# A gate broadcast moved behind four transposes, and scale columns regrouped, in a DiT block on one core

## The chip, the cores and the metric

The kernel runs on one core of a Trainium2 chip. The metric is the device time of that core in microseconds.

The engines are called as the profile calls them: PE is the matmul engine, PEld its weight loads, DVE, ACT and POOL the vector, scalar and GpSimd engines, SP the engine that issues most loads.

## The reference, cut to what matters

```python
# B, N, D = 2, 256, 1152; H = 2 heads of 576; F = 4608; all bfloat16
mod = (silu(c) @ w_mod).reshape(B, 6, 1, D)
shift_a, scale_a, gate_a, shift_m, scale_m, gate_m = [mod[:, i] for i in range(6)]
h = layernorm(x) * (1 + scale_a) + shift_a
q, k, v = h @ wqkv                                    # cut: reshapes
attn = softmax(q k^T * Dh ** -0.5)
x = x + gate_a * ((attn @ v) @ wo)
h2 = layernorm(x) * (1 + scale_m) + shift_m
out = x + gate_m * (gelu(h2 @ w_fc1) @ w_fc2)
```

D is nine blocks of 128. "Column j of the scale" below means block j of `scale_a`, which is needed before the normalized activations of block j can be modulated and used in K step j.

## The kernel before

Everything is resident or streamed through five large weight buffers, and PE works from start to end.

**The first loads**, on SP's queue, in the order in which PE will want them: scale columns and rows of the K weights, alternating.

```python
SGROUPS = [(0, 2), (2, 4), (4, 6), (6, 8), (8, 9)]
for k0, k1 in SGROUPS:
    nc.sync.dma_start(w_scale_a[:, :, k0*P:k1*P], ...)     # one load for each group of columns
    for a, z in [(0, 1), (1, 2)] if k0 == 0 else [(k0, k1)]:
        load_k(a, z, 0, KM1 * P)                           # rows of the K weights
load_k(0, KD, KM1 * P, D)
```

**The K steps.** `scale_group` computes columns by small matmuls, `transpose_x` and `modulate` make block k of the activations, `k_step` accumulates it into six PSUM tiles.

```python
k_step(0, N, T)                      # batch 1's half of step 0
pm = scale_group(2, 4)               # waits for the second scale load
pt_b = transpose_x([2, 3], BT[0])
scale_add(pm, 2, 4)
modulate(...)                        # cut: DVE and ACT
k_step(1, N, T)                      # batch 1's half of step 1
...                                  # cut
for k in range(3, KD):
    split = 2 if k == 5 else 0
    k_step(k, 0, T, 0, split)
    if k in (3, 5, 7):
        k1 = min(k + 3, KD)
        scale_add(scale_group(k + 1, k1), k + 1, k1)
    ...                              # cut
```

**Attention.** Four softmaxes end in four DMA transposes on ACT's queue (`transposed` is the last). The gate vector is written to a DRAM tile in four pieces and read back broadcast to 128 partitions, 2 x 288 KB, on POOL's queue. The next weights (`w_shift_m`, `w_scale_m`, `w_f1_0`, a first piece of `w_f1_1`) wait for the last transpose.

```python
def gate_natural_finish(g, pn):
    ...                                            # cut: four small writes to gates_dram
    return broadcast_gate(g)                       # two DMAs, at once
for i, (pnl, t) in enumerate(v_order):
    if i < len(softmaxes):
        transposed = softmaxes[i]()
    if i == 0:
        gate_a = gate_finish()
    v_group(pnl, t)
w_shift_m = load_rows("w_shift_m", ...)
tc.add_manual_dep(first_load["w_shift_m"], transposed.ins.name, WAIT_FOR, reason="transposes first")
w_scale_m = load_rows(...); w_f1[0] = load_rows(...)
for c0, c1 in ((0, PW), (PW, D)):                  # two pieces of w_f1_1; the second waits for LN2
    load = nc.sync.dma_start(w_f1[1][:, :, c0:c1], ...)
```

**The second layernorm (LN2).** Each token tile t is normalized, then turned by a DMA transpose on ACT's queue into `hT`. fc1 of batch 0 needs tiles 0 and 1. It follows the output projection ("wo") on PE directly.

```python
nc.scalar.dma_start_transpose(hT[:, :, t * P:(t + 1) * P], xn2[:])
```

Of the kernel before, what the change touches and what calls it, by code (L numbers as in the profile page):

```python
# [19 lines left out]
def kernel(  # L20
# [11 lines left out]
    nc = tc.nc  # L32
    B, N, D = x.shape
# [3 lines left out]
    P = 128  # L37
    T = B * N
    NT = T // P
    TPB = N // P  # L40
    KD = D // P
# [8 lines left out]
    WAIT_FOR = mybir.DependencyInfo(mybir.DependencyClass.Sync, mybir.DependencyReason.DATA)  # L50
# [9 lines left out]
    def acc_tile(shape, name, dt=FP32):  # L60
        return psum.tile(shape, dt, name=name, tag="acc", bufs=6)
# [16 lines left out]
    def wide_tile(name):  # L78
        return wide.tile([P, KD, D], BF16, name=name, tag="wide")
# [15 lines left out]
    sT = act.tile([P, KD, SW], BF16, name="sT")  # L95
    nc.gpsimd.memset(sT[:], 0.0)

    SGROUPS = [(0, 2), (2, 4), (4, 6), (6, 8), (8, 9)]
    KM1 = 6
    w_scale_a = wide_tile("w_scale_a")  # L100
    w_k = wide_tile("w_k")
# [1 line left out]
    def load_k(k0, k1, c0, c1):  # L103
        nc.sync.dma_start(w_k[:, k0:k1, c0:c1], wqkv_v[:, k0:k1, D + c0:D + c1])

    for k0, k1 in SGROUPS:
        nc.sync.dma_start(
            w_scale_a[:, :, k0 * P:k1 * P],
            wmod_v[:, :, S_SCALE_A * D + k0 * P:S_SCALE_A * D + k1 * P],
        )  # L110
        for a, z in [(0, 1), (1, 2)] if k0 == 0 else [(k0, k1)]:
            load_k(a, z, 0, KM1 * P)
    load_k(0, KD, KM1 * P, D)

# [2 lines left out]
    def load_rows(name, view, col0):  # L117
        w = wide_tile(name)
        for r in range(0, KD, 3):
            load = nc.sync.dma_start(w[:, r:r + 3, :], view[:, r:r + 3, col0:col0 + D])  # L120
            first_load.setdefault(name, load.ins)
        return w
# [109 lines left out]
    def norm1(t, c0, c1):  # L232
        nc.vector.tensor_scalar(
            xns[t][:, c0:c1], x_sb[:, t, c0:c1], mv1[:, t, 0:1], rstd1[:, t:t + 1],
            op0=ALU.subtract, op1=ALU.mult,
        )
# [4 lines left out]
    def scale_group(k0, k1, tile_of=aux_tile):  # L241
        pm = tile_of([P, k1 - k0, B], "pm")
        for j in range(k0, k1):
            if j == 0:
                nc.tensor.matmul(pm[:, 0, :], ones_row[:], ones_row[:, 0:B], start=True, stop=False)
            for k in range(KD):
                nc.tensor.matmul(  # L247
                    pm[:, j - k0, :], w_scale_a[:, k, j * P:(j + 1) * P], sT[:, k, 0:B],
                    start=(k == 0 and j > 0), stop=(k == KD - 1),
                )  # L250
        return pm

    def scale_add(pm, k0, k1, eng="d"):
        if eng == "a":
            nc.scalar.activation(scale_a[:, k0:k1, :], pm[:], ACT.Identity, bias=ones[:])
        else:
            nc.vector.tensor_scalar_add(scale_a[:, k0:k1, :], pm[:], 1.0)

    def transpose_x(ks, ts, pt=None, j0=0):
        if pt is None:  # L260
            pt = aux_tile([P, len(ks), len(ts) * P], "pt", BF16)
        for j, t in enumerate(ts, j0):
            for i, k in enumerate(ks):
                nc.tensor.transpose(pt[:, i, j * P:(j + 1) * P], xns[t][:, k * P:(k + 1) * P], ident[:])  # L264
        return pt
# [10 lines left out]
    def k_step(k, c0=0, c1=T, m0=0, m1=KM1):  # L276
        for m in range(m0, m1):
            if k == 0 and c0 == 0:
                pk[m] = acc_tile([P, T], "pk")
            nc.tensor.matmul(  # L280
                pk[m][:, c0:c1], w_k[:, k, m * P:(m + 1) * P], hT0[:, k, c0:c1],
                start=(k == 0 and c0 == 0), stop=(k == KD - 1), skip_group_check=True,
            )
# [33 lines left out]
    def both(pt, k):  # L317
        for b, e in enumerate("da"):
            modulate(pt, 0, k, b, b * N, e)
# [60 lines left out]
    norm1(0, CUT, D)  # L380
    norm1(1, CUT, D)
    k_step(0, N, T)
    pm = scale_group(2, 4)
    pt_b = transpose_x([2, 3], BT[0])
    scale_add(pm, 2, 4)
    modulate(pt_b, 0, 2, 0, 0, "d")
    modulate(pt_b, 1, 3, 0, 0, "a")
    norm1(2, CUT, D)
    k_step(1, N, T)
    pt_d = transpose_x([2, 3], BT[1])  # L390
    modulate(pt_d, 0, 2, 1, 0, "d")
    modulate(pt_d, 1, 3, 1, 0, "a")
    norm1(3, CUT, D)
    k_step(2, 0, N)
    k_step(2, N, T)
    for k in range(3, KD):
        split = 2 if k == 5 else 0
        k_step(k, 0, T, 0, split)
        if k in (3, 5, 7):
            k1 = min(k + 3, KD)  # L400
            scale_add(scale_group(k + 1, k1), k + 1, k1)
        if k < KD - 1:
            both(transpose_x([k + 1], range(NT)), k + 1)
        k_step(k, 0, T, split)
# [45 lines left out]
    nc.vector.tensor_reduce(fold[:], ident[:].rearrange("p (q a) -> p a q", a=32), axis=AX.X, op=ALU.add)  # L450
    gates_dram = tc.dram_tile([2, B, D], BF16, name="gates_dram")

    def broadcast_gate(g):
        gate = act.tile([P, B, D], BF16, name="gate", tag="gate")
        for b in range(B):
            nc.gpsimd.dma_start(gate[:, b, :], gates_dram[g, b:b + 1, :].partition_broadcast(P))
        return gate


# [23 lines left out]
    def gate_vector_finish(g, folded):  # L483
        rows = D // 32
        pg = aux_tile([rows, B, 32], "pg")
        for b in range(B):
            nc.tensor.matmul(pg[:, b, :], folded[:, b, :], fold[:], start=True, stop=True)
        nat = work.tile([rows, B, 32], BF16, name="nat_v", tag="nat_v", bufs=1)
        nc.vector.tensor_copy(nat[:], pg[:])  # L489
        for b in range(B):  # L490
            nc.gpsimd.dma_start(gates_dram[g, b, :].rearrange("(j r) -> j r", r=32), nat[:, b, :])  # L491
        return broadcast_gate(g)

    def gate_natural(g, wg):
        pn = aux_tile([P, CTW], "pg")
        for k in range(KD):
            for i in range(4):
                nc.tensor.matmul(  # L498
                    pn[32 * i:32 * i + B, :], sT[:, k, 0:B], wg[:, k, i * CTW:(i + 1) * CTW],
                    start=(k == 0), stop=(k == KD - 1), tile_position=(0, 32 * i),  # L500
                )
        return lambda: gate_natural_finish(g, pn)

    def gate_natural_finish(g, pn):
        nat = work.tile([P, CTW], BF16, name="nat", tag="nat", bufs=1)
        for i in range(4):
            rows = slice(32 * i, 32 * i + B)
            if i % 2 == 0:
                nc.vector.tensor_copy(nat[rows, :], pn[rows, :])  # L509
            else:  # L510
                nc.scalar.copy(nat[rows, :], pn[rows, :])
            nc.gpsimd.dma_start(gates_dram[g, :, i * CTW:(i + 1) * CTW], nat[rows, :])  # L512
        return broadcast_gate(g)


    pq = [None] * KD
# [54 lines left out]
    gate_finish = gate_natural(0, w_gate_a)  # L571
# [24 lines left out]
    def v_group(pnl, t):  # L596
        pacc = acc_tile([P, PW], "pacc")
        for k in range(KD):
            nc.tensor.matmul(  # L599
                pacc[:], hT[:, k, t * P:(t + 1) * P], w_v[:, k, pnl * PW:(pnl + 1) * PW],  # L600
                start=(k == 0), stop=(k == KD - 1),
            )
        evac(v_sb[:, t, pnl * PW:(pnl + 1) * PW], pacc[:])
# [3 lines left out]
    for i, (pnl, t) in enumerate(v_order):  # L607
        if i < len(softmaxes):
            transposed = softmaxes[i]()
        if i == 0:  # L610
            gate_a = gate_finish()
        v_group(pnl, t)

    w_shift_m = load_rows("w_shift_m", wmod_v, S_SHIFT_M * D)
    tc.add_manual_dep(first_load["w_shift_m"], transposed.ins.name, WAIT_FOR, reason="transposes first")
    w_scale_m = load_rows("w_scale_m", wmod_v, S_SCALE_M * D)
    w_f1[0] = load_rows("w_f1_0", wfc1_v, 0)
    w_f1[1] = wide_tile("w_f1_1")
    for c0, c1 in ((0, PW), (PW, D)):
        load = nc.sync.dma_start(w_f1[1][:, :, c0:c1], wfc1_v[:, :, D + c0:D + c1])  # L620
# [172 lines left out]
    for gi, (n, t, c0, cw) in enumerate(groups):  # L793
        b = t // TPB
# [59 lines left out]
```

## Time and profile before

| | before |
|---|---|
| time, median of 3 runs | 243.91 us (243.87 to 244.05) |
| span of the profiled execution | 241.8 us |
| PE busy | 235.4 us |
| first real matmul | 8.8 us |
| last matmul's start | 238.4 us |

From the page of the profile: the span, the busy time by engine, and the chain of work that ended last, as shares of the span by engine.

```profile
span 241.8 us, 3979 instructions
...
PE 235.4 (97%) x1688; PEld 144.4 (60%) x1698; DVE 91.5 (38%) x193; ACT 59.9 (25%) x121; POOL 28.3 (12%) x47
...
PE 94%; issue 2%; ACT 2%; POOL 1%; DVE 0%; POOLq 0%; DVEq 0%; ACTq 0%
```

PE is the bound. The view of windows gives the length of a stretch and the busy time of PE, PEld, DVE, ACT and POOL in it, then the granted clock, the DMA share and GB/s.

```profile
8.80:25.50 16.70, 16.27 (x189) 11.13 (x191) 7.36 (x25) 6.14 (x14) 0.98 (x3) 1.00 1.13 320
56.00:97.70 41.70, 41.70 (x329) 26.32 (x330) 25.48 (x62) 13.57 (x37) 9.86 (x13) 1.00 0.88 272
```

The first row is the stage of scale groups and K steps: 0.43 us are idle. The second row is from the v matmuls to fc1: nothing is idle.

The waits view, for PE alone (who waited for whom: us in total, times, longest):

```profile
PE pt L264 <- DVE xn L233: 1.5, 2, 1.2
PE pwarm L173 <- DVE eps_t L93: 1.2, 1, 1.2
```

No matmul waits for a load. The timeline (start, length, engine, line, operation) shows the weight loads of the second scale group running without a wait:

```profile
12.69 0.61 PEld L247 LDWEIGHTS <-w_scale_a 128*128 128x128 bf16 x18
```

The timeline around the attention transposes: the third and fourth transpose, the two broadcasts, and the load of w_shift_m that waits for the fourth transpose.

```profile
61.33 2.55 ACTq L550 DMA_TRANSPOSE soft<-soft  x2
63.26 1.14 POOL L456 DMA_DIRECT2D gate<-gates_dram  x2 [1.86 <-DMA gates_dram<-nat]
67.06 0.90 SPq L120 DMA_DIRECT2D w_shift_m<-in_w_mod_dram  x2
```

The view of the tile, cut to the fourth transpose, gives its time from issue to landing:

```profile
L550 ACTq DMA_TRANSPOSE soft<-soft x1: 1242/1242/1242, 62.6 to 62.6; - x1
...
DMA to landing us min/median/max: 4.4/4.4/4.4
```

And the timeline where wo ends and fc1 begins: the second LN2 transpose is issued, DVE modulates, PE starts fc1.

```profile
93.66 1.31 ACTq L681 DMA_TRANSPOSE hT<-xn  x1
96.98 0.60 DVE L662 TENSOR_SCALAR hT<-hT,scale_m,shift_m 128x256 bf16<-128x256 bf16 x2 [0.26 <-DMA hT<-xn]
97.62 0.60 PE L743 MATMUL pacc<-hT,w_f 128*128 128x256 bf16 x4
```

PE has no idle time in front of it, as the view of windows shows for this place:

```profile
96.50:98.00 1.50, 1.50 (x12) 1.01 (x11) 1.24 (x5) 1.22 (x4) 0.47 (x1) 1.00 0.00 0
```

### The profile page before, as it was taken

What the parts mean: (1) busy time and instruction counts of PE and PEld (TensorE: products, weight loads), DVE (VectorE), ACT (ScalarE), POOL (GpSimd) and SP (SyncE); (2) the same over time, 40 slices, a digit from 0 to 9 for tenths busy, and PEclk for the clock granted to TensorE, in tenths of its full rate; (3) what the DMA queues carried; (4) which work ended last, traced back from release to release, by engine and by line L of the source; (5) the groups of instructions that cost most, each with busy time, mean ns of one, the idle gap of its engine ahead of it and who ended that gap; (6) DMA issues with size and microseconds to landing.
All of it is one profiled execution on the core that took longest, in us unless ns stands there. A gap on an engine that the chain in (4) does not pass through costs nothing.

```text
span 241.8 us, 3979 instructions
## 1 busy us (share of the span) xinstructions
PE 235.4 (97%) x1688; PEld 144.4 (60%) x1698; DVE 91.5 (38%) x193; ACT 59.9 (25%) x121; POOL 28.3 (12%) x47
## 2 busy tenths in 40 slices
PE   8799999999999999999999999999999999999994
PEld 5585444465567566888844444444556665566674
DVE  3742442319325678830002999960010000000001
ACT  6633322307215032671422333222000000000000
POOL 2300000002300324100000000001121111111111
PEclk9999999999999999999999999999999999999999
DMA  6999999997579999239999999999200000000000
GB/s 188 327 317 310 378 366 393 389 391 247 147 263 398 387 377 159 49 59 361 391 391 391 340 327 284 274 327 284 98 16 16 20 16 16 19 18 19 27 23 16
DMA packets 48781, 53.29 MB, mean 220 GB/s; under 512 B 9587, under 2 KB 36475, under 8 KB 48763
## 3 DMA queue, kind: packets, MB, share of 16 engines
q1 hardware_dynamic: 41312, 50.14, 62.5%
q10 hardware_dynamic: 6939, 1.71, 4.7%
q0 software_dynamic: 512, 1.19, 1.5%
q8 instruction: 13, 0.21, 0.4%
q14 instruction: 5, 0.04, 0.0%
HBM read 50.14 MB, written 1.19 MB: 212 GB/s over the span
## 4 chain that ended last, share of the span: by engine, by line
PE 94%; issue 2%; ACT 2%; POOL 1%; DVE 0%; POOLq 0%; DVEq 0%; ACTq 0%
PE pacc L799 29%; PE pacc L743 29%; PE pacc L690 7%; PE pacc L599 7%; PE pq L521 7%; PE pk L280 5%; PE pk L309 2%; PE pa L639 2%; PE ps_s L556 2%; PE pn L416 2%; ACT sink L206 1%; PE pt L264 1%; PE pm L247 1%; PE pg L498 0%; ACT rstd L335 0%
## 5 line engine op out<-in xcount | busy, mean ns | idle before, releaser
L743 PE MATMUL pacc<-hT,w_f 128*128 128x256 bf16 (+1 forms) x427 | 70.3, 325 | 0.3
L799 PE MATMUL pacc<-w_f,gT 128*128 128x384 bf16 (+2 forms) x468 | 70.5, 314 | 0.0
L799 PEld LDWEIGHTS <-gT 128*128 128x128 bf16 x468 | 44.4, 98 | 26.2
L743 PEld LDWEIGHTS <-w_f 128*128 128x128 bf16 x432 | 42.2, 98 | 27.6
L805 DVE TENSOR_TENSOR tmp<-pacc,gate 128x384 f32<-128x384 f32 (+2 forms) x13 | 6.9, 527 | 65.6 <-PE pacc L799 57.2
L775 ACT ACTIVATE gT<-pacc 128x512 bf16<-128x512 f32 x24 | 14.3, 597 | 32.6 <-PE pacc L743 32.6
L469 DVE SCALAR_TENSOR_TENSOR part<-w_gate_m,s,part 128x1152 f32<-128x1152 bf16 x16 | 21.4, 1414 | 0.0
L807 POOL TENSOR_TENSOR o_sb<-tmp,x 128x384 bf16<-128x384 f32 (+1 forms) x12 | 11.7, 973 | 54.0 <-DVE tmp L805 54.0
L690 PE MATMUL pacc<-w_o,big 128*128 128x384 bf16 x108 | 17.9, 326 | 0.0
L521 PE MATMUL pq<-hT,w_q 128*128 128x512 bf16 x79 | 17.7, 379 | 0.1
L599 PE MATMUL pacc<-w_v,hT 128*128 128x384 bf16 x108 | 17.7, 326 | 0.0
L599 PEld LDWEIGHTS <-hT 128*128 128x128 bf16 x108 | 10.5, 98 | 7.1 <-issue 0.3
L690 PEld LDWEIGHTS <-big 128*128 128x128 bf16 x108 | 10.4, 98 | 7.2 <-issue 0.4
L521 PEld LDWEIGHTS <-w_q 128*128 128x128 bf16 x81 | 7.9, 98 | 9.4
L280 PE MATMUL pk<-big,w_k 128*128 128x256 bf16 (+1 forms) x70 | 13.1, 324 | 0.1
L696 POOL TENSOR_TENSOR x<-tmp,x_sb 128x384 f32<-128x384 f32 x8 | 7.3, 914 | 27.4 <-DVE tmp L695 27.4
L467 DVE TENSOR_SCALAR part<-w_gate_m,s 128x1152 f32<-128x1152 bf16 x2 | 1.6, 818 | 22.3 <-DMA w_gate_m<-in_w_mod_dram 22.3
L491 POOL DMA_DIRECT2D gates_dram<-nat_v x2 | 1.1, 536 | 67.7 <-DVE nat_v L489 67.7
L280 PEld LDWEIGHTS <-w_k 128*128 128x128 bf16 x72 | 6.7, 97 | 3.7 <-issue 0.3
L764 ACT ACTIVATE gT<-pacc 128x512 bf16<-128x512 f32 x12 | 6.5, 598 | 8.9 <-PE pacc L743 8.9
L512 POOL DMA_DIRECT2D gates_dram<-nat x4 | 2.3, 584 | 49.3 <-DVE nat L509 48.7
L695 DVE TENSOR_TENSOR tmp<-pacc,gate 128x384 f32<-128x384 f32 x12 | 6.6, 549 | 3.1 <-PE pacc L690 3.1
(102 smaller groups left out, 164.2 us busy)
## 6 DMA issues: line engine op xcount, KB each, us to landing
w_f<-in_w_fc_dram SPq DMA_DIRECT2D x12, 864.0 KB, 14.9
w_f<-in_w_fc_dram SPq DMA_DIRECT2D x3, 1728.0 KB, 7.9
w_f<-in_w_fc_dram SPq DMA_DIRECT2D x2, 2592.0 KB, 17.2
w_gate_a<-in_w_mod_dram SPq DMA_DIRECT2D x3, 864.0 KB, 11.9
w_v<-in_wqkv_dram SPq DMA_DIRECT2D x3, 864.0 KB, 13.8
w_o<-in_wo_dram SPq DMA_DIRECT2D x3, 864.0 KB, 14.0
w_shift_m<-in_w_mod_dram SPq DMA_DIRECT2D x3, 864.0 KB, 6.6
w_scale_m<-in_w_mod_dram SPq DMA_DIRECT2D x3, 864.0 KB, 12.1
```

Of the source, the lines that this page charges most:

```text
L280: nc.tensor.matmul(pk[m][:, c0:c1], w_k[:, k, m * P:(m + 1) * P], hT0[:, k, c0:c1], start=(k == 0 and c0 == 0), stop=(k == KD - 1), skip_g ...
L469: nc.vector.scalar_tensor_tensor(part[:, b, :], wg[:, k, :], s32[:, k, b:b + 1], part[:, b, :], op0=ALU.mult, op1=ALU.add,)
L521: nc.tensor.matmul(pq[m][:], w_q[:, k, m * P:(m + 1) * P], hT[:, k, :], start=(k == 0), stop=(k == KD - 1), skip_group_check=True,)
L599: nc.tensor.matmul(pacc[:], hT[:, k, t * P:(t + 1) * P], w_v[:, k, pnl * PW:(pnl + 1) * PW], start=(k == 0), stop=(k == KD - 1),)
L690: nc.tensor.matmul(pacc[:], aT[:, k, t * P:(t + 1) * P], w_o[:, k, c0:c1], start=(k == 0), stop=(k == KD - 1),)
L695: nc.vector.tensor_tensor(tmp[:], pacc[:], gate_a[:, b, c0:c1], op=ALU.mult)
L696: (nc.gpsimd if pool_add else nc.vector).tensor_tensor(x1[:, t, c0:c1], tmp[:], x_sb[:, t, c0:c1], op=ALU.add)
L743: nc.tensor.matmul(dst, w_f1[m // KD][:, k, ml * P:(ml + 1) * P], hT[:, k, c0:c1], start=start, stop=(k == KD - 1), **kw,)
L775: nc.scalar.activation(gT[:, m, :], pacc[:], ACT.Gelu_apprx_tanh)
L799: nc.tensor.matmul(pacc[:], gT[:, kk, t * P:(t + 1) * P], w_f2[j][:, r, c0 - n * PW:c0 - n * PW + cw], start=(kk == 0), stop=(kk == KF - 1),)
L805: nc.vector.tensor_tensor(tmp[:], pacc[:], gate_m[:, b, c0:c0 + cw], op=ALU.mult)
L807: (nc.vector if last else nc.gpsimd).tensor_tensor(o_sb[:], tmp[:], x1[:, t, c0:c0 + cw], op=ALU.add)
```

## The change

The intent can be read from the diff. The broadcast no longer shares the DMA engines with the last attention transpose, so the transpose and the loads behind it come earlier. The scale columns come in four loads instead of five, without the narrow last one. Three matmuls go ahead of the second group, whose load is now larger.

```diff
-    SGROUPS = [(0, 2), (2, 4), (4, 6), (6, 8), (8, 9)]
+    SGROUPS = [(0, 2), (2, 5), (5, 7), (7, 9)]
@@
-        for a, z in [(0, 1), (1, 2)] if k0 == 0 else [(k0, k1)]:
+        ends = {0: (1, 2), 2: (3, 5)}.get(k0, (k1,))
+        for a, z in zip((k0,) + ends, ends):
             load_k(a, z, 0, KM1 * P)
@@
     k_step(0, N, T)
+    k_step(1, N, T, 0, 3)
     pm = scale_group(2, 4)
     pt_b = transpose_x([2, 3], BT[0])
@@
-    k_step(1, N, T)
+    k_step(1, N, T, 3)
@@
+    INSIDE = {3: (0, (4, 5)), 4: (2, (5, 7)), 6: (2, (7, 9))}
     for k in range(3, KD):
-        split = 2 if k == 5 else 0
+        split, group = INSIDE.get(k, (0, None))
         k_step(k, 0, T, 0, split)
-        if k in (3, 5, 7):
-            k1 = min(k + 3, KD)
-            scale_add(scale_group(k + 1, k1), k + 1, k1)
+        if group:
+            scale_add(scale_group(*group), *group)
@@
-    def broadcast_gate(g):
+    def broadcast_gate(g, behind=None):
         gate = act.tile([P, B, D], BF16, name="gate", tag="gate")
         for b in range(B):
-            nc.gpsimd.dma_start(gate[:, b, :], gates_dram[g, b:b + 1, :].partition_broadcast(P))
+            load = nc.gpsimd.dma_start(gate[:, b, :], gates_dram[g, b:b + 1, :].partition_broadcast(P))
+            if behind is not None:
+                tc.add_manual_dep(load.ins, behind, WAIT_FOR, reason="transposes first")
+                behind = None
@@ gate_natural_finish
-        return broadcast_gate(g)
@@
-            gate_a = gate_finish()
+            gate_finish()
@@
     tc.add_manual_dep(first_load["w_shift_m"], transposed.ins.name, WAIT_FOR, reason="transposes first")
+    gate_a = broadcast_gate(0, transposed.ins.name)
     w_scale_m = load_rows("w_scale_m", wmod_v, S_SCALE_M * D)
```

## The prediction

> **What bounds it.** TensorE. The page gives PE 235.4 us busy of a 241.8 us span; the chain of waits is 94% PE. After warm-up's start the waits view lists two PE waits, both for normalized activations (1.5 us together), none for a DMA. The rest is the start (first real matmul at 8.82 us) and the tail (3 us). In the stretch 8.8 to 25.5 us, where scale groups and K steps run, PE is busy 16.27 of 16.70 us: at most 0.43 us to give. From 56.0 to 97.7 us PE has no idle time.
>
> **Change 1: scale groups.** All scale columns and K matmuls stay; order and load sizes change. Landings, from issue start plus time to landing: group 2-3 about 12.1 us (interpolated), group 4-5 at 15.26, 6-7 at 18.32, 8 at 21.33. PE's weight loads ask for them at 12.69, 15.55, 19.36, 22.46: slack 0.6, 0.3, 1.0, 1.1 us. Nothing waits today. After: group 2-4 has 864 KB instead of 576; at about 300 KB/us (group 4-5: 576 KB in 1.96 us) it lands near 13.0 us. Three 256-column matmuls (0.33 us in the chain) now go first, so PE asks at about 13.02. Slack shrinks to nearly zero: a stall of 0 to 0.3 us is possible. Later groups gain: 5-6 lands near 16.7, wanted near 18.0; 7-8 near 19.8 against 21.5. The lone column 8 with its 256-byte pieces is gone; it took 1.19 us for 288 KB (242 KB/us, against about 295 for 512-byte pieces). The Trainium skill, "DMA: Bandwidth & Descriptors", Specifications, puts line rate at 512 bytes or more; this trace agrees. That saves about 0.25 us of queue time, off the critical path.
> The moved matmuls leave 0.33 us less cover for the next modulation: VectorE's would end near 14.37, wanted at 14.51. Tight, but no wait.
>
> **Change 2: gate_a.** Now its two broadcasts (issued 63.26 and 63.8 us, landing after 3.6 to 3.8) overlap the last attention transpose, which takes 4.4 us against 2.4 to 2.5 for those before it, and holds w_shift_m's load until 67.06. After: that transpose lands about 2 us earlier, w_shift_m is issued near 65, and the broadcast shares the DMA engines with it, landing near 69 to 71. Its first reader runs at 79.31: 8 us of slack. The broadcast's traffic (about 1.5 us at 390 GB/s) moves into the busy load phase, cancelling most of the 2 us. w_scale_m lands today at 84.2, wanted at 87.6; it should land at most 0.5 us earlier. PE has no idle time here: gain on the span zero.
>
> **Prediction.** 243.9 us, range 243.5 to 244.5. Faster by over 2%: 0.4%; within 2%: 99%; slower: 0.6%.
>
> **What would show it.** Right: PE busy near 235.4; no PE wait for DMA, or one below 0.3 us at the second scale group (12.7 to 13.5 us); last attention transpose under 3 us; w_shift_m issued near 65 us; first gate product still released by PE near 79.3. Wrong: a gate product waiting for the gate; a PE gap above 0.3 us near 13 us; fc1 starting later than 97.6 us plus any shift from the K steps.
>
> **What would make it wrong.** Group 2-4 landing later than 13.3 us, each further 0.1 us adding 0.1; landings in unprofiled runs that differ, so that before really stalls at group 4-5 and after gains some tenths; the broadcast starving behind the load queue; loads running longer into the LN2 transposes before 97 us.

## The result, and the profile after

| | before | after |
|---|---|---|
| time, median of 6 runs | 243.89 us (243.55 to 244.41) | 243.88 us (243.80 to 244.67) |
| ratio, 95% interval | | 1.0003 (0.9986 to 1.0019) |
| span of the profiled execution | 241.8 us | 242.2 us |
| PE busy | 235.4 us | 235.6 us |

A ratio here and below is the mean time of one kernel's fast runs over the mean of the other's fast runs of the same rounds, so it isn't quite the ratio of the medians quoted.

The time is the same. The profile is not: nearly each thing that the change was to do happened. The page:

```profile
span 242.2 us, 3979 instructions
...
PE 235.6 (97%) x1688; PEld 144.1 (60%) x1698; DVE 91.5 (38%) x193; ACT 60.2 (25%) x121; POOL 28.3 (12%) x47
...
PE 91%; issue 2%; ACT 2%; DMA 2%; DVE 1%; POOL 1%; DVEq 0%; POOLq 0%; ACTq 0%
```

The chain of work that ended last now has 2% DMA in it, where before it had none. The windows of the first stretch, and of the place where wo ends and fc1 begins:

```profile
8.80:25.50 16.70, 16.34 (x188) 10.91 (x188) 7.11 (x25) 5.91 (x13) 0.74 (x3) 1.00 1.11 336
96.50:98.00 1.50, 1.39 (x10) 0.76 (x8) 0.71 (x3) 0.98 (x3) 0.50 (x1) 1.00 0.36 78
```

In the first stretch PE is as busy as it was. In the second it is idle for 0.11 us where before had none. (From 56.00 to 97.70 us nothing is idle in this kernel either; that stretch ends just before the gap.) The weight loads of the second scale group now wait for their load, 0.23 us by the timeline, and begin at 13.02 us, close to the 13.0 us that the prediction gave for the larger load's landing:

```profile
13.02 0.52 PEld L248 LDWEIGHTS <-w_scale_a 128*128 128x128 bf16 x18 [0.23 <-DMA w_scale_a<-in_w_mod_dram]
```

(PE itself waits 0.17 us for the first scale load, at 9.26 us; the change leaves that load as it was.)

The attention transposes, w_shift_m's load and the broadcast on the timeline:

```profile
61.36 2.53 ACTq L554 DMA_TRANSPOSE soft<-soft  x2
65.12 1.43 SPq L121 DMA_DIRECT2D w_shift_m<-in_w_mod_dram  x3
65.64 1.14 POOL L458 DMA_DIRECT2D gate<-gates_dram  x2 [4.21 <-DMA soft<-soft]
```

The fourth transpose's time to landing in the view of its tile:

```profile
L554 ACTq DMA_TRANSPOSE soft<-soft x1: 1231/1231/1231, 62.7 to 62.7; - x1
...
DMA to landing us min/median/max: 2.4/2.4/2.4
```

The fourth transpose takes 2.4 us instead of 4.4, and w_shift_m's load goes out 1.94 us earlier. The gate is read for the first time at 79.34 us and is still released by PE, as before.

But the timeline at the start of fc1 has this:

```profile
93.69 1.31 ACTq L686 DMA_TRANSPOSE hT<-xn  x1
...
97.53 0.60 DVE L667 TENSOR_SCALAR hT<-hT,scale_m,shift_m 128x256 bf16<-128x256 bf16 x2 [0.78 <-DMA hT<-xn]
97.92 0.27 PE L748 MATMUL pacc<-hT,w_f 128*128 128x256 bf16 x1
```

The second LN2 transpose was issued 0.03 us later than before and landed at 97.43 instead of 96.88 us. fc1 starts 0.30 us later. That is most of the 0.37 us between the two spans (242.16 and 241.79 us exactly). The question for the experiments is whether that is noise, which part of the change makes it, and why loads that started 2 us earlier end up hurting.

### The profile page after: what moved, and what is told of

Same layout as the page of the kernel before. It is cut to its first block, busy times and chain, and to the rows that moved or that the text cites. A ratio compares the mean times of both kernels' runs of the same rounds, so it can differ in the third digit from the quotient of the medians.

```text
span 242.2 us, 3979 instructions
## 1 busy us (share of the span) xinstructions
PE 235.6 (97%) x1688; PEld 144.1 (60%) x1698; DVE 91.5 (38%) x193; ACT 60.2 (25%) x121; POOL 28.3 (12%) x47
## 3 DMA queue, kind: packets, MB, share of 16 engines
q0 software_dynamic: 512, 1.19, 1.7%
HBM read 50.14 MB, written 1.19 MB: 212 GB/s over the span
## 4 chain that ended last, share of the span: by engine, by line
PE 91%; issue 2%; ACT 2%; DMA 2%; DVE 1%; POOL 1%; DVEq 0%; POOLq 0%; ACTq 0%
PE pacc L804 29%; PE pacc L748 29%; PE pacc L603 7%; PE pq L525 7%; PE pk L281 5%; PE pacc L695 4%; PE pk L310 2%; PE pa L644 2%; PE ps_s L560 2%; DMA hT<-xn 2%; PE pn L418 2%; ACT sink L207 1%; PE pt L265 1%; PE pm L248 1%; PE pg L503 0%
## 5 line engine op out<-in xcount | busy, mean ns | idle before, releaser
L804 PEld LDWEIGHTS <-gT 128*128 128x128 bf16 x468 | 44.3, 98 | 26.3
L603 PEld LDWEIGHTS <-hT 128*128 128x128 bf16 x108 | 10.5, 98 | 7.1 <-issue 0.3
## 6 DMA issues: line engine op xcount, KB each, us to landing
w_o<-in_wo_dram SPq DMA_DIRECT2D x3, 864.0 KB, 13.9
```

The lines of the kernel that those rows point to most:

```text
L603: nc.tensor.matmul(pacc[:], hT[:, k, t * P:(t + 1) * P], w_v[:, k, pnl * PW:(pnl + 1) * PW], start=(k == 0), stop=(k == KD - 1),)
L804: nc.tensor.matmul(pacc[:], gT[:, kk, t * P:(t + 1) * P], w_f2[j][:, r, c0 - n * PW:c0 - n * PW + cw], start=(kk == 0), stop=(kk == KF - 1),)
```

## The experiments

There were twelve runs in three sets of four (e1 to e4; r1, e6, e7, e8; e5, e9, r2, r3), each set on one chip with its own runs of the kernel before. The changed kernel itself was timed again in the second set only, so a comparison of the other two sets with it goes through the ratios to before. Each run had one profile and five rounds. All results were correct.

| run | what it is | ratio to before (95%) | medians, this / before |
|---|---|---|---|
| e1_gate_only | before + gate part | 1.0020 (1.0004 to 1.0036) | 244.05 / 243.63 |
| e2_groups_only | before + groups part | 1.0039 (1.0020 to 1.0058) | 244.65 / 243.63 |
| e3_split_load | after, 864 KB load in two | 1.0029 (1.0015 to 1.0044) | 244.34 / 243.63 |
| e4_no_move | after, three matmuls not moved | 1.0042 (1.0025 to 1.0058) | 244.46 / 243.63 |
| r1_after_again | after, unaltered | 1.0002 (0.9983 to 1.0020) | 243.98 / 243.93 |
| e6_gate_twice | after, broadcast doubled | 1.0043 (1.0020 to 1.0066) | 245.13 / 243.93 |
| e7_late_piece | after, piece of w_f1_1 held | 1.0003 (0.9983 to 1.0024) | 244.10 / 243.93 |
| e8_late_piece_before | before, piece held | 0.9987 (0.9970 to 1.0003) | 243.65 / 243.93 |
| e5_bigger_group | after, second group 1152 KB | 1.0054 (1.0042 to 1.0066) | 244.62 / 243.53 |
| e9_groups_late_piece | groups only, piece held | 1.0007 (0.9995 to 1.0020) | 243.66 / 243.53 |
| r2_groups_again | groups only again | 1.0046 (1.0029 to 1.0062) | 244.58 / 243.53 |
| r3_late_before_again | before, piece held, again | 1.0015 (0.9997 to 1.0033) | 243.76 / 243.53 |

The second table is worked out from the trace of each run, in us. "Loads" is the time from the issue of w_shift_m to the landing of the third piece of w_f1_0. "Lag" is the landing of the second LN2 transpose minus the start of the last wo matmul. "Gap" is the start of the first fc1 matmul minus the start of the last wo matmul, less the 0.16 that remains where nothing waits. The profile's own idle figures, counted from the modelled end of the last matmul, come out about 0.16 us smaller than this gap.

| run | 4th attention transpose | w_shift_m issued | broadcast among the loads | loads | lag | gap |
|---|---|---|---|---|---|---|
| before | 4.37 | 67.06 | no | 23.9 | -0.58 | 0 |
| e8, r3 | 4.31, 4.77 | 67.08, 67.28 | no | 24.2, 24.2 | -0.58, -0.58 | 0, 0 |
| e2, r2 | 5.13, 4.99 | 68.24, 68.49 | no | 24.1, 24.2 | 0.45, 0.63 | 0.79, 0.97 |
| e9 | 5.24 | 67.95 | no | 24.1 | -0.57 | 0 |
| after, r1 | 2.41, 2.41 | 65.12, 64.97 | once | 26.4, 26.3 | -0.06, 0.15 | 0.28, 0.48 |
| e1 | 2.39 | 65.18 | once | 26.2 | -0.34 | 0 |
| e3, e4 | 2.39, 2.41 | 65.31, 65.66 | once | 26.3, 26.5 | -0.32, -0.12 | 0.02, 0.22 |
| e5 | 2.41 | 65.98 | once | 26.3 | 0.37 | 0.70 |
| e7 | 2.41 | 64.80 | once | 26.4 | -0.55 | 0 |
| e6 | 2.41 | 65.30 | twice | 29.4 | 1.24 | 1.58 |

### Each part alone: e1_gate_only and e2_groups_only

e1 takes the gate part of the diff above and leaves the groups. e2 takes the rest; as a diff against the changed kernel:

```diff
@@ gate_natural_finish
+        return broadcast_gate(g)
@@
-            gate_finish()
+            gate_a = gate_finish()
@@
-    gate_a = broadcast_gate(0, transposed.ins.name)
```

> The kernel before with the gate part of the change alone. My theory (each part touches only slack): the last attention transpose lands in 2.4 us instead of 4.4, w_shift_m is issued near 65.1, no scale group waits for a load, the gate is read for the first time at 79.3 still released by PE; time within 0.15% of before. In the changed kernel's profile the second LN2 transpose landed 3.7 us after its issue instead of 3.2 and PE sat 0.27 us before fc1; if the gate's later traffic is the cause, this run has the gap too (0.1 to 0.4 us). Rival A (two real effects that cancel): this run is slower than before by 0.2 to 0.4 us (ratio 1.001 to 1.002) and the groups-only run faster by as much. Rival B (noise of one profile): no gap before fc1 here.

> The changed kernel with gate_a's broadcast where it was before. My theory: PE waits 0.1 to 0.3 us for the load of scale columns 2-4 near 13 us, as in the changed kernel; the last attention transpose takes 4.4 us again and w_shift_m goes out near 67; no gap before fc1 (under 0.05 us); time within 0.15% of before, if anything 0.1 to 0.2 us slower. Rival A: faster than before by 0.2 to 0.4 us. Rival B: a gap before fc1 may show here as well.

My theory held for e1's transpose and lost in most of the rest. e1's fourth transpose took 2.39 us and w_shift_m went out at 65.18, as expected, but PE has no gap before fc1 there, and the ratio, 1.0020, is outside the 0.15% that I gave. It is e2, with the broadcast in its old place, that has the gap, and a larger one. In e2 the transpose took 5.13 us and not 4.4, w_shift_m went out at 68.24 and not near 67, and the ratio was 1.0039. The expected wait at the second scale group did not show in e2: PE came to the group only at 13.42 us. From the timeline of e2:

```profile
94.08 1.33 ACTq L686 DMA_TRANSPOSE hT<-xn  x1
...
98.83 1.03 PE L748 MATMUL pacc<-hT,w_f 128*128 128x256 bf16 x8 [0.62 <-DVE hT L667]
```

Rival A had foreseen two effects of opposite sign, with groups-only the faster one. Both parts alone came out slower than before, by 0.20% (an interval that just excludes 1) and 0.39%. For the changed kernel, which has both, the first measurement's interval (0.9986 to 1.0019) lies below that of groups-only (1.0020 to 1.0058). So the parts aren't a sum: the gate part takes back most of what the groups part loses. Gate-only and the changed kernel can't be told apart. The second table shows where the parts meet. In e2 the fourth attention transpose, with the broadcast beside it, took 5.13 us, w_shift_m went out at 68.24 us, and the loads, which took 24.1 us as before, ended 1.36 us later than before (92.31 against 90.95 us). The LN2 transposes followed them. Of the 1.36 us, 0.42 are not the transpose's: this profile was already late when the v matmuls began (56.35 against 55.93 us). The column "lag" doesn't hold that shift.

### The changed kernel again: r1_after_again

> The changed kernel itself, unaltered, beside before on the chip and in the rounds of the runs below. My theory after the first four runs: before fc1 there is a chain (end of the load queue, then the two LN2 transposes of batch 0, then the first modulation, then PE) with only some 0.2 us of slack in before; the change delays the end of that queue by about 1 us and uses the slack up. So this profile again shows the second LN2 transpose landing about 0.2 us before PE could start, and a PE gap of 0.1 to 0.5 us before fc1; ratio to before between 1.000 and 1.003. Rival (noise of one profile): no gap this time.

The gap came again, larger. From this run's timeline, the start of fc1:

```profile
97.97 1.80 PE L748 MATMUL pacc<-hT,w_f 128*128 128x256 bf16 x15 [0.32 <-DVE hT L667]
```

So it isn't the chance of one profile, and rival B falls. The ratio, 1.0002, repeats the first result, 1.0003.

### What the broadcast costs the loads: e6_gate_twice

```diff
     gate_a = broadcast_gate(0, transposed.ins.name)
+    spare = act.tile([P, B, D], BF16, name="spare", tag="spare")
+    for b in range(B):
+        nc.gpsimd.dma_start(spare[:, b, :], gates_dram[0, b:b + 1, :].partition_broadcast(P))
```

> The changed kernel with the two broadcasts of gate_a issued a second time, to a spare tile that nobody reads. It doubles the suspected cost. In before the loads from w_shift_m to the first piece of w_f1_1 took 28.1 us from first issue to last landing, in the changed kernel with the broadcast among them 31.1 us: the broadcast cost 3.0 us of load time, twice what its bytes take at 390 GB/s (1.5 us). Theory: a second one costs 3 us again, the last piece lands near 99 us, the second LN2 transpose near 100, and PE gets a gap before fc1 of 2 to 3 us: ratio about 1.01. If it costs its bytes only: 1.5 us, a gap of 1.2 to 1.8 us, ratio about 1.006. Rival (the LN2 transposes don't wait for the loads): no gap beyond 0.3 us, ratio under 1.003.

From the timeline of e6, the start of fc1:

```profile
99.40 0.38 PE L751 MATMUL pacc<-hT,w_f 128*128 128x256 bf16 x2 [1.41 <-DVE hT L670]
```

The gap was 1.58 us by the table and the ratio 1.0043, so the forecast of 2 to 3 us and 1.01 failed. The gap lies in the range that I had given for "its bytes only", and the last landing in front of the LN2 transposes came 1.8 us later than in r1 (97.97 against 96.22 us). The column "loads", which stops one load earlier, gives more. Without a broadcast among them the same loads took 23.9 to 24.2 us in six profiles (mean 24.1); with one, 26.2 to 26.5 us in seven (mean 26.3); with two, 29.4 us. So one broadcast cost about 2.2 us of load time (2.5 between the first two profiles) and the second 3.1 us, not the 1.5 us that its bytes would take at 390 GB/s.

Where the rest comes from is in the windows of the profiles. For most of the time that the broadcast ran, all DMA traffic together was slower than the loads are alone. First before, then the changed kernel; the last number is GB/s:

```profile
71.00:72.50 1.50, 1.50 (x11) 0.88 (x9) 0.28 (x1) 0.24 (x1) 0.00 (x0) 1.00 1.03 393
```

```profile
69.50:71.00 1.50, 1.50 (x11) 0.92 (x10) 0.39 (x1) 0.21 (x1) 0.00 (x0) 1.00 1.12 316
71.00:72.50 1.50, 1.50 (x11) 0.90 (x10) 0.24 (x1) 0.27 (x1) 0.00 (x0) 1.00 0.91 261
```

Before moved 406 and 393 GB/s in these 3 us, the changed kernel 316 and 261. The missing 0.33 MB are 0.85 us at 390 GB/s; with the 1.5 us of the bytes that is an estimate of 2.4 us. The profile of before already showed such a rate: from 65.0 to 66.5 us, with the broadcast, the fourth attention transpose and no load running, its DMA engines moved 261 GB/s. Why a broadcast is slower is not shown.

The last landing mixes in the LN2 transposes, which run in the same time at the end of the queue: the second of them landed only 1.43 us later than in r1 (98.90 against 97.47 us).

The Trainium skill, "DMA: Bandwidth & Descriptors", section "Issuing engines are not separate DMA queues", says that DMAs issued by different engines run on the same 16 DMA engines and interleave. This agrees: a broadcast on POOL's queue delays loads on SP's queue by about 2.2 us and, through them, transposes on ACT's.

### Taking the queue's tail away: e7, e9, e8 and r3

The first piece of w_f1_1 (864 KB) is the last load in front of the LN2 transposes. PE wants it near 106 us. The same edit holds it until the second LN2 transpose has landed, in the changed kernel (e7), in groups-only (e9) and in before (e8, r3):

```diff
     for c0, c1 in ((0, PW), (PW, D)):
         load = nc.sync.dma_start(w_f1[1][:, :, c0:c1], wfc1_v[:, :, D + c0:D + c1])
+        if c0 == 0:
+            w_f1_1_first = load.ins
@@ ln2_normalize
-        nc.scalar.dma_start_transpose(hT[:, :, t * P:(t + 1) * P], xn2[:])
+        turned = nc.scalar.dma_start_transpose(hT[:, :, t * P:(t + 1) * P], xn2[:])
+        if t == 1:
+            tc.add_manual_dep(w_f1_1_first, turned.ins.name, WAIT_FOR, reason="transposes first")
```

> The changed kernel with the first piece of w_f1_1 (864 KB, wanted by PE from about 106 us) held until the second LN2 transpose has landed. It shortens the load queue ahead of the LN2 transposes by about 2.3 us. Theory: the first LN2 transpose lands 1 to 3 us earlier than 96.6, the second near 95 to 96.5, the gap before fc1 goes (PE's first fc1 matmul within 0.05 us of the end of the wo matmuls), the piece lands near 102, in time; span 0.2 to 0.3 us shorter than the changed kernel's. Rival (the transposes are slow by themselves, loads or not): the second transpose still lands 3.7 us after its issue and the gap stays.

> The groups-only kernel (gate_a's broadcast in its old place) with the first piece of w_f1_1 held until the second LN2 transpose has landed. The groups-only run was slower than before, 1.0039, and its profile had a PE gap of 0.62 us before fc1. Theory (that gap is most of its loss): the gap goes, ratio to before between 0.999 and 1.002. Rival (its loss lies in the K stage): the gap goes and the ratio stays near 1.004.

> The groups-only kernel once more, to be compared with the run above on the same chip. Theory: ratio 1.002 to 1.005; last attention transpose 4.4 to 5.2 us, w_shift_m issued after 67 us, a PE gap before fc1 of 0.2 to 0.7 us. Rival (its 1.0039 was chance of the first set): ratio under 1.0015 and no gap.

The timeline of e7, second LN2 transpose and start of fc1:

```profile
93.36 1.31 ACTq L688 DMA_TRANSPOSE hT<-xn  x1
...
97.32 2.46 PE L752 MATMUL pacc<-hT,w_f 128*128 128x256 bf16 x21
```

The same of r2, which ran in the same rounds as e9:

```profile
94.48 1.32 ACTq L686 DMA_TRANSPOSE hT<-xn  x1
...
99.41 0.38 PE L748 MATMUL pacc<-hT,w_f 128*128 128x256 bf16 x2 [0.80 <-DVE hT L667]
```

And of e9:

```profile
93.69 1.31 ACTq L688 DMA_TRANSPOSE hT<-xn  x1
...
97.64 2.13 PE L752 MATMUL pacc<-hT,w_f 128*128 128x256 bf16 x18
```

In e7 and e9 the gap is gone, as expected. The first LN2 transpose landed at 92.10 and 92.96 us (96.60 in r1, 98.07 in r2; in e7 that is 4.5 us earlier, where I gave 1 to 3), the second at 96.61 and 96.91, the held piece at 101.63 and 101.89, in time. So the lateness of the transposes was the loads' doing. For groups-only the timed runs confirm it: r2 repeated the loss at 1.0046, and e9 beside it was at 1.0007. Nearly the whole loss of groups-only is this gap. (The two profiles differ by more than the gap, since r2's profiled execution also started late: its first scale load landed at 9.99 us, e9's at 9.21.)

For the changed kernel they confirm nothing: e7 was at 1.0003 and r1 beside it at 1.0002. The profiled execution was the shortest of all twelve (241.56 us), but its timed runs spread from 243.34 to 244.49. A gap of 0.3 to 0.5 us is a ratio of 1.001 to 1.002, as wide as these intervals.

> The kernel before with the same hold on the first piece of w_f1_1: a candidate that might beat both kernels. Before's profile showed no gap before fc1, so theory: same time as before within 0.1% (ratio 0.998 to 1.001), unless before's unprofiled slower runs (244.0 to 244.4) have that gap, in which case those go and the mean falls by 0.1 to 0.3 us. Rival (loads don't matter to the transposes): no change at all in the landings.

> The kernel before with the held piece once more (first time 0.9987, interval 0.997 to 1.0003): is it faster than both kernels? Theory: before's slack before fc1 is about 0.4 us in its profile and is used up in some of its executions, so the hold gains 0.1 to 0.3 us in the mean: ratio 0.9985 to 0.9995, and no gap before fc1 in the profile. If the ratio is 1.000 or more, the first result was chance.

In before the hold moved the first LN2 transpose from 95.72 to 92.14 and 93.85 us, and the second from 96.88 to 96.97 and 96.71, because the second is issued only at 93.5 to 93.8 and takes 3.2 us even alone. The ratios were 0.9987 and then 1.0015, both with intervals that hold 1. The second is outside what I expected. No gain is shown, and my idea that the gap is what makes before's slow executions slow has no support. No version here beats both kernels.

### The second scale group: e4_no_move, e5_bigger_group and e3_split_load

```diff
-    k_step(1, N, T, 0, 3)
     pm = scale_group(2, 4)
@@
-    k_step(1, N, T, 3)
+    k_step(1, N, T)
```

> The changed kernel without moving the three matmuls of K step 1 ahead of scale group 2-3: all six stay behind the transposes, as before. My theory: PE asks for the 864 KB load 0.33 us earlier, so its wait near 13 us grows from 0.23 to about 0.55 us, and the span is 0.3 us longer than the changed kernel's; the cover for the modulation behind is 0.33 us more, which is worth nothing. Rival (the move only shifts the wait, the load isn't the limit): the wait stays near 0.2 us and the time is the changed kernel's.

The weight loads of the group in the timeline of e4:

```profile
13.31 0.52 PEld L248 LDWEIGHTS <-w_scale_a 128*128 128x128 bf16 x18 [0.84 <-DMA w_scale_a<-in_w_mod_dram]
```

The wait of the weight loads grew from 0.23 to 0.84 us, where I expected 0.55. The difference is the load, which was usable 0.29 us later in this profile (13.31 against 13.02 us); its first scale load was late already (9.46 against 9.21 us). PE itself sat idle 0.56 us at the group, by the same view for PE; in the changed kernel no idle time of PE is listed at this place. Less the late load, about 0.3 us remain that the moved matmuls hide. The v matmuls began at 56.50 us against 55.96, of which I expected 0.3.

```diff
-    SGROUPS = [(0, 2), (2, 5), (5, 7), (7, 9)]
+    SGROUPS = [(0, 2), (2, 6), (6, 7), (7, 9)]
@@
-        ends = {0: (1, 2), 2: (3, 5)}.get(k0, (k1,))
+        ends = {0: (1, 2), 2: (3, 6)}.get(k0, (k1,))
```

> The changed kernel with the second load of scale columns made still bigger: columns 2-5 in one load of 1152 KB (then column 6, then 7-8), all else as it is. The same columns are computed at the same places. Theory (PE waits for the whole load of the group, at about 300 KB/us, and nothing later takes the wait back): it lands about 0.95 us later than the 864 KB one, near 13.9 us, PE's wait there is 1.0 to 1.3 us instead of 0.2, and the span is 0.8 to 1.1 us longer than the changed kernel's: ratio near 1.004. Rival (later waits shrink by as much, the K stage being limited by the stream of loads as a whole): v's first matmul comes at most 0.3 us later than the changed kernel's 55.9 to 56.0.

The same weight loads in the timeline of e5:

```profile
13.88 0.49 PEld L248 LDWEIGHTS <-w_scale_a 128*128 128x128 bf16 x17 [0.89 <-DMA w_scale_a<-in_w_mod_dram]
```

The group began at 13.88 us, against the 13.9 worked out from 300 KB/us, and the v matmuls at 56.82 us, 0.86 us later than in the changed kernel. The weight loads waited 0.89 us and PE itself was idle 0.62 us, both less than the 1.0 to 1.3 that I gave; 0.2 us of the shortfall is that PE's own work came to the group later in this execution (the transposes ahead of it at 11.40 against 11.20 us). The ratio is 1.0054; a gap of 0.70 us before fc1 adds to the wait. So the stage takes nothing back later, and the slack in front of the second group is what the load's size is paid from.

```diff
     for k0, k1 in SGROUPS:
-        nc.sync.dma_start(w_scale_a[:, :, k0 * P:k1 * P], ...)
+        for s0, s1 in ([(2, 4), (4, 5)] if k0 == 2 else [(k0, k1)]):
+            nc.sync.dma_start(w_scale_a[:, :, s0 * P:s1 * P], ...)
```

> The changed kernel with the 864 KB load of scale columns 2-4 issued as two, columns 2-3 and then column 4. My theory: columns 2-3 land near 12.1 us, so the PE wait near 13 us goes (under 0.05 us); K steps end 0.2 us earlier against the first transposes; column 4 in 256-byte pieces lands near 13.4 and is wanted at 15.5, no wait. Span at most 0.2 us shorter than the changed kernel's, which the timing can hardly tell. Rival (the wait is not for this load's size): the wait stays.

The wait at 13 us went, as expected: the group's weight loads began at 12.67 us. But the timeline of e3 has two new waits further on:

```profile
19.58 1.41 PEld L282 LDWEIGHTS <-w_k 128*128 128x128 bf16 x8 [0.22 <-DMA w_k<-in_wqkv_dram]
...
21.55 0.52 PEld L249 LDWEIGHTS <-w_scale_a 128*128 128x128 bf16 x18 [0.56 <-DMA w_scale_a<-in_w_mod_dram]
```

The wait moved to the last group, whose load landed at 21.51 us, against 20.44 in the changed kernel's profile. The v matmuls began at 56.17, not earlier than the changed kernel's 55.96. Column 4 alone comes in 256-byte pieces, as column 8 did in before. The Trainium skill, "DMA: Bandwidth & Descriptors", Specifications, gives 512 bytes as the least for line rate; in before 288 KB of such pieces took 1.19 us. Loads of 512-byte pieces moved 576 KB in 1.96 us there, which agrees. In e3 k row 2 landed at 14.07 against 13.50 us. But the extra load also takes time on SP's queue: the last group's load was issued at 12.72 us against 11.91, and that is 0.81 of the 1.07 us by which it landed later. Which of the two it is, the pieces' size or the extra load, no run separates.

## Why the prediction was right

- **The time.** 243.88 us against 243.9, within the range. That PE is the bound and nothing on PE was removed, so that there is no gain, is what happened: PE busy moved from 235.4 to 235.6 us. But some of it is luck. The prediction named as a sign of being wrong "fc1 starting later than 97.6 us plus any shift from the K steps", and that came true: 97.92 us, with a shift of 0.03 us (v matmuls at 55.96 against 55.93). The gap is too small for the timed runs to tell. And the prediction did not foresee that the groups part alone loses 0.4%, most of which the gate part makes good.
- **The second scale group.** Right. Its weights were usable at 13.02 us, as worked out, and the wait by the weight loads was 0.23 us of the 0 to 0.3 foreseen. (They asked for them at 12.79 and not at 13.02, since PE had come through the work before 0.2 us earlier than in before's profile.) e4 and e5 show both terms: the move hides about 0.3 us, and the wait grows with the load's size.
- **The later groups.** Right in direction: columns 5-6 landed at 16.59 (16.7 predicted) and columns 7-8 at 20.44 (19.8 predicted, 0.6 us off), both ahead of use.
- **The transposes and w_shift_m.** Right: 2.41 us and an issue at 65.12 us.
- **The gate's landing.** Wrong in size: 72.55 and 75.12 us instead of 69 to 71. It still lands 4 us before its first reader, so nothing came of it.
- **The broadcast's cost to the loads.** This is the term that was mis-sized: "about 1.5 us at 390 GB/s ... cancelling most of the 2 us". That is the rate of the loads, and no broadcast ran at it: with the broadcast among them, all transfers together fell to 261 to 316 GB/s. It cost about 2.2 us of load time (2.5 between these two profiles), so it more than cancelled the 1.94 us, and the loads ended 0.5 us later instead of up to 0.5 us earlier (third piece of w_f1_0 at 91.48 against 90.95 us).
- **"PE has no idle time here: gain on the span zero."** True of a gain, but a loss was possible, and I gave it one clause among the risks. What decides it is a chain beside PE: loads, LN2 transposes, modulation, fc1. From the table the gap opens when the lag passes about -0.34 us (at -0.34 and -0.32 there is 0 and 0.02, at -0.12 there is 0.22), and above that each further 0.1 us of lag is 0.1 us of gap. Before stands at -0.58, so its slack is some 0.24 us. The changed kernel's two profiles are past it by 0.28 and 0.48 us.
- **How the two parts hang together.** Groups-only loses 0.4% twice, and holding one piece of the tail repairs it (e9). The gate part does some of the same repair in another way: it lets w_shift_m go out 3 us earlier than in groups-only and pays about 2.2 us for it. That is shown by the issues and the loads column. The gap falls by some 0.5 us (0.79 and 0.97 to 0.28 and 0.48), while the ratios differ by 0.4%, about 0.9 us; the other half is not accounted for, though the intervals are wide enough to hold it. This is also why the change can't be judged by its parts.

What stays open. The profiles of the changed kernel are 0.37 and 0.41 us longer than that of before; the timed runs, with intervals of 0.17 to 0.19% either way (0.4 to 0.5 us), can't tell this from zero. Gate-only's 1.0020 has no gap in its profile to explain it; its lag is just at the edge, so that some executions may have one, but that isn't shown. The loads' end alone doesn't fix the gap: in the six profiles with the broadcast once and nothing held, the third piece of w_f1_0 landed 5.9 to 6.2 us before the last wo matmul, while the lag went from -0.34 to 0.37 us in no such order. There the second LN2 transpose landed 1.24 to 1.28 us after the first piece of w_f1_1 each time, and it is this piece, beside the transposes, that landed 4.5 us after the piece before it in one profile and 5.2 in another; why is open. And it is unexplained why the broadcast beside the fourth transpose is slower in the three kernels with the new groups (transpose 5.0 to 5.2 us, the broadcast's 4608-byte packets 281 to 306 ns on the mean) than in the three with the old ones (4.3 to 4.8 us, 222 to 267 ns).

## What to carry to other kernels

When PE is busy in every stretch, look for the chains that run beside it and write down by how much each one wins, since it is there that a change that moves DMA traffic can lose. Moving a transfer out of the way of one thing puts it in the way of the next: cost it by what it delays and by the rate at which the profile shows it to run, and not by its bytes at the rate of other loads. Test the parts of a change together as well as apart, because slack that one part uses may be what the other part supplies.

## What the Trainium skill lacked or had wrong

- The Trainium skill, "DMA: Bandwidth & Descriptors", Rules for kernel authors, says that a transpose next to ordinary DMAs needs nothing. That is about correct results, and the results here were correct. What the page lacks is the cost: the same attention transpose took 2.4 us alone and 4.3 to 5.2 us beside a 2 x 288 KB broadcast, and the first LN2 transpose landed 8.4 to 10.5 us after its issue behind loads, against 4.7 to 6.7 us with the last 864 KB of them held.
- The Trainium skill, "Advanced Engine Details and Errata", X-Bar Transpose (TRN2), says that transpose DMAs are as fast as regular ones. No run here compares the two directly; what is missing on that page is how a transpose fares beside the traffic of other queues, with the numbers above.
- The same DMA page, "Queues, rings and completion order", has each DMA engine go round between the queues that have work. In the changed kernel the broadcast's first packet started at 69.81 us, 4.2 us after its issue at 65.64, with loads running from 66.1 us; in before, without them, 1.3 us after its issue. It was 4.0 to 4.2 us in all eight profiles with the loads running and 1.3 us in all six without. The page's Specifications give about 1 us to the first byte on this path. The page lacks how long a GpSimd-issued transfer can take to start beside loads from SP; that it is the loads that hold it up was not tested apart.
- No page has the cost of a partition broadcast from DRAM: 0.59 MB of it cost other loads about 2.2 us here, and a second one 3.1 us, where its bytes at 390 GB/s would take 1.5 us.
